# W_k and W_q transposed by blocks of 128 rows, and another order of the work ahead of the first k tile

## The chip, the cores and the metric

The kernel runs on one NeuronCore of a Trainium2 chip. PE (TensorE) does the matmuls and transposes into PSUM, ACT (ScalarE), DVE (VectorE) and POOL (GpSimd) the elementwise work, and SP (SyncE) issues every DMA of this kernel from one queue. The metric is the device time of one execution in microseconds, lower is better. Nine executions of the kernel before gave a median of 279.61 us (279.39 to 280.89).

## The reference

One layer over x of 2048 rows and 640 columns: an attention with a feature map in place of the softmax over keys, then a gated feed-forward block. There are 32 heads of 20 columns.

```python
pq = einsum("bhsd,hdf->bhsf", q, w_phi); pk = einsum("bhsd,hdf->bhsf", k, w_phi)
phi_q = concat([softmax(pq), softmax(-pq)]); phi_k = concat([softmax(pk), softmax(-pk)])
kv = einsum("bhsf,bhsd->bhfd", phi_k, v);  z = einsum("bhsf->bhf", phi_k)
o = einsum("bhqf,bhfd->bhqd", phi_q, kv) / (einsum("bhqf,bhf->bhq", phi_q, z)[..., None] + 1e-6)
h = x + o.reshape(B, S, D) @ wo                              # q, k, v = layernorm(x) @ wqkv
out = h + (gelu(layernorm(h) @ w_gate) * (layernorm(h) @ w_up)) @ w_down
```

## The kernel before

Rows are worked on in 16 tiles of 128 (four tiles make a block of 512; `x_sb[b]` holds one block of x, `LN1T[b]` its normalized transpose). For a tile t the steps are: statistics (`ln_st`, L108 and L112, with the reciprocal deviation on ACT at L117/L118 or on POOL at L120/L121), the normalization `ln_ap` (L137 on DVE, L132 on ACT), the transpose into `LN1T` (`ln_tp`: five PE transposes into PSUM at L145 and a copy at L146; for tiles 6 to 15 a DMA transpose at L148), the v projection (`v_mm`, L260, or its pieces `v_part`, L276; ten matmuls of 128x320) with its copy `v_ev` into `vS` on ACT (L280), and the k projection (`k_tile`, L260) with two exponentials on ACT (L292).

W_k and W_q are not used as they are. `fold` multiplies the weight by a block-diagonal matrix `BD` built from `w_phi`, so that one projection gives pk or pq at once. For this the weight is loaded transposed (`WkT`, `WqT`), six matmuls for each of its five blocks of 128 rows run at L224, and the result is copied to `Wk2` or `Wq2` by ACT (L233) or DVE (L235); the tuples `KA` and `QA` name the blocks that ACT copies. `BD` is one DVE multiplication of `wphi` with the mask `hmask` (L391).

The order on PE and SP is the program's; nothing is reordered there, nor on the other engines, since the whole body stands in a hand-written schedule. Ahead of the loop over tiles (L414) stands a prologue (L374 to L409): tiles 0 to 5 are normalized, tiles 0 to 4 transposed on PE, v is made of tiles 0 to 3, and W_k is folded in two stretches, one in the middle of v of tile 3. In the loop each turn t makes k of tile t and v of tile t + 4; the transposes of tile 5 stand in turn 0 ahead of v of tile 4, and one W_q block is folded in each of the turns 4 to 8 (`FQ`). Tile 3's statistics are made on ACT by two passes (`st3_act`, L357: the squares and the plain sum) and finished on POOL (L359 to L363).

The SP queue begins with x rows by pieces, Wv in three pieces (L174, L176, L177), wphi (L178), then x of tiles 4 and 5 (L179), W_k's transposition as one DMA (L180), x of tiles 6 and 7 (L181), of tiles 8 to 11 (L185), W_q's transposition as one DMA (L186), and x of tiles 12 to 15 (L187). After these come the ten DMA transposes of tiles 6 to 15. [...]

`gtile` takes a PSUM buffer of two banks from a pool of four (three from turn 4 on, with the fourth for `kvp`); a new tile takes the buffer that came free first in the program's order, and its first matmul waits for the last reader of the tile before.

Of the kernel before, what the change touches and what calls it, by code (L numbers as in the profile page):

```python
# [10 lines left out]
ALU = mybir.AluOpType  # L11
# [6 lines left out]
def kernel(  # L18
# [12 lines left out]
    nc = tc.nc  # L31
    P = 128
    S = 2048
    D = 640
    H = 32
    Dh = 20
# [3 lines left out]
    NC = D // P  # L40
# [5 lines left out]
    NH = [(P * c + P - 1) // Dh - H0[c] + 1 for c in range(NC)]  # L46
    NWARM = 10
    VP = (0, 2, 4, 6, 9, 11)
    KA, QA = (0,3), (0,1,2,3,4)
    FQ = (4, 5, 6, 7, 8)  # L50

    QG = ((0, 1), (2, 3), (4, 5), (6,), (7, 8), (9, 10), (11, 12), (13, 14), (15,), (16,), (17,), (18,), (19,))
# [10 lines left out]
    x_v = A_x.rearrange("b (p t) d -> p (b t) d", t=NT)  # L63
    o_v = out.rearrange("b (p t) d -> p (b t) d", t=NT)
    w_v = A_wqkv.rearrange("(c p) n -> p c n", p=P)
    phi_v = A_w_phi.rearrange("h d f -> (h d) f")
# [8 lines left out]
    x_sb = [const.tile([P, 4, D], BF16, name=f"x_sb{b}") for b in range(NB)]  # L75
    wphi = const.tile([P, NC, Dh], BF16, name="wphi")
# [7 lines left out]
    hmask = const.tile([P, NC, 8], BF16, name="hmask")  # L84
    kmask = const.tile([P, NC, 4], BF16, name="kmask")
    BD = const.tile([P, NC, 8, Dh], BF16, name="BD")
# [70 lines left out]
    Wk2 = p1.tile([P, NC, D], BF16, name="Wk2")  # L157
# [16 lines left out]
    nc.sync.dma_start(Wv[:, 0:2, :], w_v[:, 0:2, 2 * D:3 * D])  # L174
    nc.sync.dma_start(x_sb[0][:, 2:3, :], x_v[:, 2:3, :])
    nc.sync.dma_start(Wv[:, 2:4, :], w_v[:, 2:4, 2 * D:3 * D])  # L176
    nc.sync.dma_start(Wv[:, 4:5, :], w_v[:, 4:5, 2 * D:3 * D])  # L177
    nc.sync.dma_start(wphi, phi_v.rearrange("(c p) f -> p c f", p=P))  # L178
    nc.sync.dma_start(x_sb[1][:, 0:2, :], x_v[:, 4:6, :])  # L179
    nc.sync.dma_start_transpose(WkT, A_wqkv[:, D:2 * D])  # L180
    nc.sync.dma_start(x_sb[1][:, 2:4, :], x_v[:, 6:8, :])  # L181
    wo_v = A_wo.rearrange("(c p) n -> p c n", p=P)
    wg_v = B_w_gate.rearrange("(c p) n -> p c n", p=P)
    wu_v = B_w_up.rearrange("(c p) n -> p c n", p=P)
    nc.sync.dma_start(x_sb[2], x_v[:, 8:12, :])  # L185
    nc.sync.dma_start_transpose(WqT, A_wqkv[:, 0:D])  # L186
    nc.sync.dma_start(x_sb[3], x_v[:, 12:16, :])  # L187


    zero = fp.tile([P, 512], BF16, name="zero")  # L190
# [19 lines left out]
    def fold(WT, W2, halves, ds=range(NC)):  # L210


        runs = []
        for c in range(NC):
            lo, hi = H0[c] * Dh, (H0[c] + NH[c]) * Dh
            for u in range(2):
                a, b = max(lo, u * HD), min(hi, (u + 1) * HD)
                if a < b:
                    runs.append((u, c, a, b))
        runs.sort()  # L220
        for d in ds:
            wa = gtile("wa")
            for i, (u, c, a, b) in enumerate(runs):
                nc.tensor.matmul(wa[:, u, a - u * HD:b - u * HD], lhsT=WT[:, c, d * P:(d + 1) * P],  # L224
                                 rhs=BD[:, c].rearrange("p a b -> p (a b)")[:, a - H0[c] * Dh:b - H0[c] * Dh],
                                 start=(i == 0 or runs[i - 1][0] != u),
                                 stop=(i + 1 == len(runs) or runs[i + 1][0] != u), skip_group_check=True)
            dst, src = W2[:, d, :].rearrange("p (u f) -> p u f", u=2), wa[:, :, 0:HD]
            if halves:
                dst = W2[:, d, :].rearrange("p (c u f) -> p u c f", c=NC, u=2)  # L230
                src = src.rearrange("p u (c f) -> p u c f", c=NC)
            if d in (QA if halves else KA):
                nc.scalar.copy(dst, src)  # L233
            else:
                nc.vector.tensor_copy(dst, src)  # L235
# [3 lines left out]
    def ln_st(*tiles, act=True, between=None, log=False):  # L239
        for t, v in zip(tiles, ln_stats(p1, [x_sb[t // 4][:, t % 4, :] for t in tiles], "1", act, between, log)):  # L240
            lnp[t] = v

    def ln_ap(t, on_act=False, on_pe=False):
        ln = (ln_act if on_act else ln_dve)(p1, "1", *lnp[t])
        if on_pe:
            lnp[t] = ln
        else:
            transpose_to(LN1T[t // 4][:, :, t % 4 * P:(t % 4 + 1) * P], ln, False)

    def ln_tp(t, on_dve=False):  # L250
        transpose_to(LN1T[t // 4][:, :, t % 4 * P:(t % 4 + 1) * P], lnp[t], True, on_dve)
# [13 lines left out]
    def v_mm(t, us=(0, 1)):  # L265
        if 0 in us:
            pv[t] = gtile("pv")
        proj(pv[t], t, Wv, us)

    def v_part(t, *cs):  # L270

        if 0 in cs:
            pv[t] = gtile("pv")
        for c in cs:
            for u in range(2):
                nc.tensor.matmul(pv[t][:, u, 0:HD], lhsT=lnT(t, c), rhs=Wv[:, c, u * HD:(u + 1) * HD],  # L276
                                 start=(c == 0), stop=(c == NC - 1))

    def v_ev(t):
        nc.scalar.copy(vS[t % 8][:, :, 0:Dh].rearrange("p (u h) f -> p u h f", u=2),  # L280
                       pv[t][:, :, 0:HD].rearrange("p u (h f) -> p u h f", f=Dh))
# [72 lines left out]
    def st3_act(i):  # L354

        xt = x_sb[0][:, 3, :]
        nc.scalar.activation(sq3, xt, (ACTF.Square, ACTF.Identity)[i], accum_out=sm3[:, i:i + 1])  # L357
        if i == 1:
            nc.gpsimd.tensor_scalar(v3[:, 0:1], sm3[:, 1:2], sm3[:, 1:2], -1.0 / (D * D), op0=ALU.mult, op1=ALU.mult)  # L359
            nc.gpsimd.tensor_scalar_add(v3[:, 0:1], v3[:, 0:1], EPS)  # L360
            nc.gpsimd.tensor_scalar(v3[:, 1:2], sm3[:, 0:1], 1.0 / D, v3[:, 0:1], op0=ALU.mult, op1=ALU.add)
            nc.gpsimd.tensor_tensor(v3[:, 2:3], v3[:, 1:2], nhalf[:, 0:1], op=ALU.pow)
            nc.gpsimd.tensor_scalar(v3[:, 3:4], sm3[:, 1:2], 1.0 / D, None, op0=ALU.mult)  # L363
            lnp[3] = xt, v3[:, 3:4], v3[:, 2:3], None
# [2 lines left out]
    sm3 = fp.tile([P, 2], F32, name="sm3")  # L367
    v3 = fp.tile([P, 4], F32, name="v3")

    def st1_between():  # L370
        st3_act(0)
        ln_ap(0, on_pe=True)

    ln_st(0, act=False, log=True)  # L374
    ln_st(1, act=False, between=st1_between, log=True)
    st3_act(1)
    ln_tp(0, True)
    warm(WA)
    ln_ap(1, on_pe=True)
    v_part(0, 0, 1)  # L380
    ln_tp(1)
    ln_st(2, act=False, log=True)
    v_part(0, 2, 3, 4)
    v_ev(0)
    v_part(1, 0, 1, 2)
    ln_ap(2, on_pe=True)
    ln_ap(3, on_pe=True)
    ln_tp(2, True)
    ln_st(4, act=False)

    nc.vector.tensor_tensor(BD, wphi[:, :, None, :].to_broadcast([P, NC, 8, Dh]),  # L391
                            hmask[:, :, :, None].to_broadcast([P, NC, 8, Dh]), ALU.mult)
    v_part(1, 3, 4)
    v_ev(1)
    v_part(2, 0, 1)
    ln_tp(3)
    v_part(2, 2, 3, 4)
    v_ev(2)
    ln_ap(4, on_pe=True)
    ln_st(5, act=False)  # L400
    v_mm(3, (0,))
    fold(WkT, Wk2, False, (0, 1))
    v_mm(3, (1,))
    v_ev(3)
    fold(WkT, Wk2, False, (2, 3, 4))
    ln_ap(5, on_pe=True)
    ln_tp(4)
    ln_st(6)
    ln_st(7)  # L409
    fp_cm.__exit__(None, None, None)  # L410
    ev_cm = tc.tile_pool(name="ev", bufs=1, side="right", reuse_waits="tile")
# [2 lines left out]
    for t in range(NT):  # L414
        if t == T3:
            ps_cm.close()
            psG = ps_cm.enter_context(tc.tile_pool(name="psG", bufs=3, space=PSUM, reuse_waits="tile"))
            psK = ps_cm.enter_context(tc.tile_pool(name="psK", bufs=1, space=PSUM, reuse_waits="tile"))
            kvp = psK.tile([P, 2, 512], F32, name="kvp")
        k_tile(t)  # L420
        if t == 0:
            ln_tp(5)
            ln_ap(6)
        if t in FQ:
            fold(WqT, Wq2, True, [i for i, f in enumerate(FQ) if f == t])
        for j in range(len(QT)):
            if t == QT[j]:
                q_mm(j)
                q_exp(j)
        if t % 2 == 1 and t >= 5:  # L430
            kv_tile(t - 5)
            kv_tile(t - 4)
        if t + 4 < NT:
            v_mm(t + 4)
        if t > 0 and t + 6 < NT:
            ln_ap(t + 6, on_act=True)
        if t + 4 < NT:
            v_ev(t + 4)
        if t % 2 == 0 and t + 8 < NT:
            ln_st(t + 8, t + 9)  # L440
        k_norm(t)
        if t == 9:
            nc.gpsimd.memset(KV, 0.0)
            nc.gpsimd.memset(kmask, 1.0)
            for r in HALF:
                nc.gpsimd.affine_select(out=kmask[r], in_=kmask[r], pattern=[[4, NC], [-Dh, 4]],
                                        compare_op=ALU.is_ge, fill=0.0, base=0, channel_multiplier=1)
                nc.gpsimd.affine_select(out=kmask[r], in_=kmask[r], pattern=[[-4, NC], [Dh, 4]],
                                        compare_op=ALU.is_ge, fill=0.0, base=Dh - 1, channel_multiplier=-1)
            nc.gpsimd.tensor_copy(KV[:, :, 0, :, KC - 1], kmask)  # L450
            nc.gpsimd.tensor_copy(KV[:, :, 1, :, 0], kmask)
        if t == 10:
            nc.sync.dma_start(Wg, wg_v)
            nc.sync.dma_start(Wo, wo_v)
            nc.sync.dma_start(Wu, wu_v)
# [282 lines left out]
```

The softmax here doesn't subtract the row's maximum and nothing guards it: scores larger than these inputs give would overflow.

## Time and profile before

| | us |
|---|---|
| median of nine executions | 279.61 |
| the profiled execution, time | 279.61 |
| its span (first to last instruction) | 277.9 |
| PE busy | 272.5 (98%) |
| DVE busy | 165.1 (59%) |
| ACT busy | 142.9 (51%) |
| POOL busy | 95.8 (34%) |
| PE busy in the first 24.0 us | 21.52 |
| SP on W_k's transposition; issue to landing | 5.42; 7.4 |
| SP on W_q's transposition; issue to landing | 5.38; 9.0 |
| SP on one 128-row transposition of tiles 6 to 15 | 1.20 |

Busy time of an engine is the sum of its instructions' time without overlaps; matmuls are pipelined and their ends are modelled, so a busy PE can still be waiting a little inside. "Issue to landing" is the time from SP's issue of a DMA to the semaphore that tells that all its data are there. The granted clock of PE was 1.00 in all stretches.

### The profile page before, as it was taken

What the parts mean: (1) busy time and instruction counts of PE and PEld (TensorE: products, weight loads), DVE (VectorE), ACT (ScalarE), POOL (GpSimd) and SP (SyncE); (2) the same over time, 40 slices, a digit from 0 to 9 for tenths busy, and PEclk for the clock granted to TensorE, in tenths of its full rate; (3) what the DMA queues carried; (4) which work ended last, traced back from release to release, by engine and by line L of the source; (5) the groups of instructions that cost most, each with busy time, mean ns of one, the idle gap of its engine ahead of it and who ended that gap; (6) DMA issues with size and microseconds to landing.
All of it is one profiled execution on the core that took longest, in us unless ns stands there. A gap on an engine that the chain in (4) does not pass through costs nothing.

```text
span 277.9 us, 5795 instructions
## 1 busy us (share of the span) xinstructions
PE 272.5 (98%) x2337; PEld 172.1 (62%) x2337; DVE 165.1 (59%) x289; ACT 142.9 (51%) x239; POOL 95.8 (34%) x211
## 2 busy tenths in 40 slices
PE   7999999999999999999999999999999999999995
PEld 2676777764655887788854555675455577444574
DVE  5799998789397776575325757322667532233222
ACT  4669999678597856365524354413446440222200
POOL 3448997685202216355301343400225230000000
PEclk9999999999999999999999999999999999999999
DMA  6996222793530021414120212221031413000011
GB/s 206 243 241 119 51 51 47 191 394 127 162 125 0 4 47 26 93 29 94 26 71 2 47 25 55 42 73 47 5 44 24 74 25 94 26 0 0 0 50 47
DMA packets 40635, 21.05 MB, mean 76 GB/s; under 512 B 33440, under 2 KB 38816, under 8 KB 40608
## 3 DMA queue, kind: packets, MB, share of 16 engines
q1 hardware_dynamic: 40608, 20.68, 29.6%
q8 instruction: 18, 0.29, 0.4%
q14 instruction: 9, 0.07, 0.1%
HBM read 10.18 MB, written 2.62 MB: 46 GB/s over the span
## 4 chain that ended last, share of the span: by engine, by line
PE 90%; DVE 3%; DMA 3%; POOL 1%; ACT 1%; issue 0%; SPq 0%; POOLq 0%
PE gu L588 38%; PE pd L609 19%; PE pq L347 8%; PE po L543 8%; PE pk L260 6%; PE pv L260 5%; PE ab L483 3%; PE kvp L325 2%; DMA LN1T<-ln 2%; DMA x_sb<-in_A_x_dram 1%; DVE stats L108 1%; DVE Wk L235 1%; DVE ln L137 1%; PE wa L224 1%; ACT sq L357 1%
## 5 line engine op out<-in xcount | busy, mean ns | idle before, releaser
L594 DVE TENSOR_TENSOR GT<-gu,g 128x512 bf16<-128x512 f32 (+1 forms) x60 | 34.4, 581 | 54.3 <-ACT g L591 54.1
L591 ACT ACTIVATE g<-gu 128x512 bf16<-128x512 f32 (+1 forms) x60 | 30.8, 513 | 69.3 <-PE gu L588 68.2
L588 PE MATMUL gu<-LN2T,Wg 128*128 128x512 bf16 (+1 forms) x300 | 61.9, 337 | 0.1
L588 PE MATMUL gu<-LN2T,Wu 128*128 128x512 bf16 (+1 forms) x300 | 61.7, 336 | 0.0
L609 PE MATMUL pd<-Wd,GT 128*128 128x320 bf16 (+2 forms) x396 | 53.8, 295 | 0.0
L609 PEld LDWEIGHTS <-GT 128*128 128x128 bf16 x396 | 38.0, 98 | 15.3 <-DVE GT L594 0.9
L588 PEld LDWEIGHTS <-Wu 128*128 128x128 bf16 x300 | 29.4, 98 | 22.6
L588 PEld LDWEIGHTS <-Wg 128*128 128x128 bf16 x300 | 28.4, 98 | 20.7
L260 PEld LDWEIGHTS <-LN1T 128*128 128x128 bf16 x290 | 27.6, 98 | 11.7 <-DMA LN1T<-ln 0.8
L307 POOL TENSOR_TENSOR vt<-vS,rs 128x672 bf16<-128x672 bf16 x22 | 29.7, 1372 | 8.5 <-DVE rs L303 8.0
L614 DVE TENSOR_TENSOR y<-pd,x_sb 128x640 bf16<-128x640 f32 (+3 forms) x18 | 13.5, 750 | 30.2 <-PE pd L609 30.2
L491 ACT COPY AB<-ab 128x704 f32<-128x704 f32 x28 | 19.6, 748 | 19.8 <-PE ab L483 19.6
L299 DVE TENSOR_REDUCE sk<-E 128x64 f32<-128x1280 bf16 x16 | 23.1, 1446 | 3.5 <-ACT E L292 3.5
L524 DVE TENSOR_TENSOR tt<-AB,w 128x1280 bf16<-128x1280 f32 x16 | 23.8, 1486 | 1.1 <-POOL w L517 0.9
L543 PE MATMUL po<-Wo,oT 128*128 128x320 bf16 x160 | 24.3, 299 | 0.0
L292 ACT ACTIVATE E<-pk 128x640 bf16<-128x640 f32 x32 | 20.9, 707 | 6.5 <-PE pk L260 6.3
L260 PE MATMUL pk<-Wk,LN1T 128*128 128x320 bf16 x160 | 24.2, 299 | 0.0
L347 PE MATMUL pq<-LN1T,Wq 128*128 128x512 bf16 x100 | 22.9, 379 | 0.0
L352 ACT ACTIVATE Eq<-pq 128x1024 bf16<-128x1024 f32 (+1 forms) x26 | 19.9, 829 | 2.4 <-PE pq L347 2.4
L260 PE MATMUL pv<-Wv,LN1T 128*128 128x320 bf16 x130 | 20.0, 299 | 0.5 <-DMA LN1T<-ln 0.5
L543 PEld LDWEIGHTS <-oT 128*128 128x128 bf16 x160 | 15.6, 98 | 7.0 <-ACT oT L146 0.3
L132 ACT ACTIVATE ln<-x_sb,v,rstd 128x640 bf16<-128x640 bf16 x14 | 12.9, 919 | 11.3 <-POOL v L571 11.1
(89 smaller groups left out, 263.1 us busy)
## 6 DMA issues: line engine op xcount, KB each, us to landing
out_dram<-y SPq DMA_DIRECT2D x15, 160.0 KB, 1.8
Wg<-in_B_w_gate_dram SPq DMA_DIRECT2D x1, 1920.0 KB, 7.8
Wu<-in_B_w_up_dram SPq DMA_DIRECT2D x1, 1920.0 KB, 15.0
Wd<-in_B_w_down_dram SPq DMA_DIRECT2D x1, 1920.0 KB, 7.9
x_sb<-in_A_x_dram SPq DMA_DIRECT2D x2, 640.0 KB, 5.4
Wo<-in_A_wo_dram SPq DMA_DIRECT2D x1, 800.0 KB, 9.4
x_sb<-in_A_x_dram SPq DMA_DIRECT2D x4, 160.0 KB, 3.0
Wv<-in_A_wqkv_dram SPq DMA_DIRECT2D x2, 320.0 KB, 4.2
```

What stands on the lines that cost most here:

```text
L260: nc.tensor.matmul(ps[:, u, 0:HD], lhsT=lnT(t, c), rhs=W[:, c, u * HD:(u + 1) * HD], start=(c == 0), stop=(c == NC - 1))
L292: nc.scalar.activation(Ek[t][:, s, :].rearrange("p (u f) -> p u f", u=2), pk[:, :, 0:HD], ACTF.Exp, scale=(1.0 if s == 0 else -1.0))
L299: nc.vector.reduce_sum(sk, Ek[t].rearrange("p s (h f) -> p (s h) f", f=Dh), axis=AX.X)
L307: eng.tensor_tensor(vt[:, s], vS[t % 8], rs[:, s * H:(s + 1) * H, None].to_broadcast([P, H, VC]), ALU.mult)
L347: nc.tensor.matmul(pqs[j][:, i, :], lhsT=Wq2[:, kc, c * P:(c + 1) * P], rhs=LN1T[b][:, kc, :], start=(kc == 0), stop=(kc == NC - 1))
L352: nc.scalar.activation(Eq[j][:, :, s, :], pqs[j][:, 0:len(QG[j])], ACTF.Exp, scale=(1.0, -1.0)[s])
L524: nc.vector.tensor_tensor(tt.rearrange("p s (h f) -> p s h f", f=Dh), num, w[:, :, :, None].to_broadcast([P, 2, H, Dh]), ALU.mult)
L543: nc.tensor.matmul(po[:, u, 0:HD], lhsT=st[t][:, c, :], rhs=Wo[:, c, u * HD:(u + 1) * HD], start=(c == 0), stop=(c == NC - 1))
L588: nc.tensor.matmul(gu[:, i, 0:n], lhsT=W[:, c, f * P:(f + 1) * P], rhs=LN2T[b][:, c, a0:a1], start=(c == 0), stop=(c == NC - 1))
L591: nc.scalar.activation(g[:, 0:n], gu[:, 0, 0:n], ACTF.Gelu_apprx_tanh)
L594: nc.vector.tensor_tensor(st[b, "g", f][:, a0:a1], gu[:, 1, 0:n], g[:, 0:n], ALU.mult)
L609: nc.tensor.matmul(pd[:, u, n0:n1], lhsT=st[b, "g", f][:, tl * P:(tl + 1) * P], rhs=Wd[:, f, u * HD + n0:u * HD + n1], start=(f == 0), sto ...
```

## The change

wphi is loaded ahead of the third piece of Wv. W_k and W_q are transposed by five DMAs of 128 rows each (`load_T`). The loads of x of tiles 6 and 7, 8 to 11 and 12 to 15 are issued after all of W_k; three W_q blocks stand between the last two of them, the fourth W_q block is issued behind tile 6's transpose and the fifth in turn 1, ahead of tile 7's. `BD` is made in two pieces, block columns 0 to 2 and 3 to 4 (`bd`), before and after the normalization of tile 2. The two ACT passes of tile 3 move behind the reciprocal deviations of tiles 1 and 2, and the normalization of tile 3 behind the statistics of tile 4. v of tile 2 is made in one stretch, then W_k's blocks 0 to 2 are folded, tile 3 is transposed, blocks 3 and 4 are folded, and v of tile 3 is made in one stretch; ACT copies blocks 1 and 3 instead of 0 and 3. Tile 5 is transposed behind v of tile 4.

```diff
-    KA, QA = (0,3), (0,1,2,3,4)
+    KA, QA = (1,3), (0,1,2,3,4)
...
     nc.sync.dma_start(Wv[:, 2:4, :], w_v[:, 2:4, 2 * D:3 * D])
+    nc.sync.dma_start(wphi, phi_v.rearrange("(c p) f -> p c f", p=P))
     nc.sync.dma_start(Wv[:, 4:5, :], w_v[:, 4:5, 2 * D:3 * D])
-    nc.sync.dma_start(wphi, phi_v.rearrange("(c p) f -> p c f", p=P))
     nc.sync.dma_start(x_sb[1][:, 0:2, :], x_v[:, 4:6, :])
-    nc.sync.dma_start_transpose(WkT, A_wqkv[:, D:2 * D])
-    nc.sync.dma_start(x_sb[1][:, 2:4, :], x_v[:, 6:8, :])
+
+    def load_T(WT, i, *ds):
+
+        for d in ds:
+            nc.sync.dma_start_transpose(WT[:, :, d * P:(d + 1) * P], A_wqkv[d * P:(d + 1) * P, i * D:(i + 1) * D])
+
+    load_T(WkT, 1, *range(NC))
...
-    nc.sync.dma_start(x_sb[2], x_v[:, 8:12, :])
-    nc.sync.dma_start_transpose(WqT, A_wqkv[:, 0:D])
-    nc.sync.dma_start(x_sb[3], x_v[:, 12:16, :])
...
-    def st1_between():
-        st3_act(0)
-        ln_ap(0, on_pe=True)
+    def bd(c0, c1):
+
+        n = c1 - c0
+        nc.vector.tensor_tensor(BD[:, c0:c1], wphi[:, c0:c1, None, :].to_broadcast([P, n, 8, Dh]),
+                                hmask[:, c0:c1, :, None].to_broadcast([P, n, 8, Dh]), ALU.mult)
 
     ln_st(0, act=False, log=True)
-    ln_st(1, act=False, between=st1_between, log=True)
-    st3_act(1)
+    ln_st(1, act=False, between=lambda: ln_ap(0, on_pe=True), log=True)
+    st3_act(0)
     ln_tp(0, True)
     warm(WA)
     ln_ap(1, on_pe=True)
     v_part(0, 0, 1)
     ln_tp(1)
     ln_st(2, act=False, log=True)
+    st3_act(1)
     v_part(0, 2, 3, 4)
     v_ev(0)
+    bd(0, 3)
+    ln_ap(2, on_pe=True)
+    bd(3, NC)
     v_part(1, 0, 1, 2)
-    ln_ap(2, on_pe=True)
-    ln_ap(3, on_pe=True)
     ln_tp(2, True)
     ln_st(4, act=False)
-
-    nc.vector.tensor_tensor(BD, wphi[:, :, None, :].to_broadcast([P, NC, 8, Dh]),
-                            hmask[:, :, :, None].to_broadcast([P, NC, 8, Dh]), ALU.mult)
+    ln_ap(3, on_pe=True)
     v_part(1, 3, 4)
     v_ev(1)
-    v_part(2, 0, 1)
-    ln_tp(3)
-    v_part(2, 2, 3, 4)
+    v_part(2, *range(NC))
     v_ev(2)
+    nc.sync.dma_start(x_sb[1][:, 2:4, :], x_v[:, 6:8, :])
+    nc.sync.dma_start(x_sb[2], x_v[:, 8:12, :])
+    load_T(WqT, 0, 0, 1, 2)
+    nc.sync.dma_start(x_sb[3], x_v[:, 12:16, :])
+    fold(WkT, Wk2, False, (0, 1, 2))
+    ln_tp(3, False)
+    fold(WkT, Wk2, False, (3, 4))
+    v_mm(3)
+    v_ev(3)
     ln_ap(4, on_pe=True)
+    ln_tp(4)
     ln_st(5, act=False)
-    v_mm(3, (0,))
-    fold(WkT, Wk2, False, (0, 1))
-    v_mm(3, (1,))
-    v_ev(3)
-    fold(WkT, Wk2, False, (2, 3, 4))
+    ln_st(6)
     ln_ap(5, on_pe=True)
-    ln_tp(4)
-    ln_st(6)
     ln_st(7)
...
         if t == 0:
-            ln_tp(5)
             ln_ap(6)
+            load_T(WqT, 0, 3)
+        if t == 1:
+            load_T(WqT, 0, 4)
...
         if t + 4 < NT:
             v_mm(t + 4)
+            if t == 0:
+                ln_tp(5)
```

## The prediction

> **What bounds the kernel now.** I read the busy table of the whole span first, then PE by stretches, then the chain of waits in order of time, then the single waits of the stretch that has any.
>
> ```profile
> 0.00:24.00 24.00, 21.52 (x163) 13.26 (x164) 19.39 (x52) 16.01 (x30) 10.67 (x39) 1.00 0.95 221
> 24.00:48.00 24.00, 24.00 (x295) 17.97 (x294) 22.55 (x38) 22.14 (x36) 20.98 (x25) 1.00 0.28 54
> ...
> 19.01 0.44 DVE ln L137
> 19.45 0.03 DVE stats L108
> 19.48 4.24 DMA LN1T<-ln
> 23.72 0.05 issue
> 23.76 1.53 PE pv L260 x10
> 25.29 1.36 PE pk L260 x10
> ```
>
> The first two lines give length, then busy time of PE, PEld, DVE, ACT and POOL, granted clock, DMA share, GB/s. From 24 us on PE never idles, and the chain from 23.76 is PE alone, 1.36 us for each group of ten 128x320 matmuls. Before 23.76 it runs through DMA, ACT, POOL and DVE. The change touches only instructions ahead of that point, two DMAs behind it, and the PSUM buffers. So its worth is by how much earlier PE begins the v of tile 6 (now 23.76) plus what it adds behind. All times "now" are starts in the trace; those of the changed kernel I work out by following each wait with these durations.
>
> ```profile
> 15.89 1.70 PE L260 MATMUL pk<-Wk,LN1T 128*128 128x320 bf16 x10
> 17.43 0.44 PE L145 MATMUL tp<-ident,ln 128*128 128x128 bf16 x5
> 17.71 1.52 PE L260 MATMUL pv<-Wv,LN1T 128*128 128x320 bf16 x10
> 19.07 1.52 PE L260 MATMUL pk<-Wk,LN1T 128*128 128x320 bf16 x10
> ...
> 23.76 0.45 PE L260 MATMUL pv<-Wv,LN1T 128*128 128x320 bf16 x2 [0.46 <-DMA LN1T<-ln]
> ...
> 26.69 1.30 ACT L292 ACTIVATE E<-pk 128x640 bf16<-128x640 f32 x2 [0.66 <-PE pk L260]
> 27.88 0.92 ACT L132 ACTIVATE ln<-x_sb,mr,rstd 128x640 bf16<-128x640 bf16 x1
> 28.68 0.70 ACT L280 CAST vS<-pv 128x640 bf16<-128x640 f32 x1
> ```
>
> k of tile 0 holds PE from 15.89 to 17.43, 1.54 us where 1.36 are needed: its fifth operand, the last Wk copy on DVE, comes at 16.56. Then v4, k1, v5, k2 follow without a gap, the last due to end at 21.78 + 1.36 = 23.14; PE waits 0.62 us more for the transposed tile 6, which landed at 23.72. That DMA took 4.24 us where most of the ten take 2.57, since it stands behind the 640 KB load of x rows 12 to 15, landed at 23.19, itself behind W_q's transposition, landed at 20.70.
>
> **The change part by part.**
>
> *wphi ahead of the last Wv piece.* The v of tile 0 follows the Wv loads closely: its third pair of matmuls begins at 7.56 (second piece landed 7.52), its fifth at 8.13 (third piece, issued 3.64, landed 8.09). wphi is 640 runs of 40 B. From 6.4 to 8.0 the DMA engines are full, and a 40 B packet takes 10 ns in the packet records: 640 x 0.010 / 16 = 0.40 us ahead of Wv. Bounds: 0 if they slip in beside; 1.5 us, the stretch over which wphi's packets lie now. I take 0.40, by the packets' own time: fifth pair at 8.53. Of that 0.31 stays: PE does the pair and three more of tile 1 (8 x 0.135) and reaches the transposes of tile 2 at 9.61 instead of 9.30, where it now waits for ln of tile 2 anyway.
>
> The Trainium skill ("DMA: Bandwidth & Descriptors", Specifications) gives 512 B as the least transfer for line rate, which speaks against a 40 B load ahead of a needed one. [...]
>
> *Block diagonals in two pieces, squares of tile 3 later.* Now one DVE instruction of 0.94 us for 800 elements at 11.24. The pieces, 480 and 320, cost by the same rate 0.56 and 0.38. The first fits into DVE's 0.67 us wait before ln of tile 2 (8.13 to 8.80), wphi being there by about 7.9; the second ends near 9.5, before the copy of tile 2 is due. Nothing on the path; without the cover 0.6. The squares (0.83 us each with their read) move behind the rstd of tiles 1 and 2: POOL's statistics of tile 3, 1.9 us, end at 11.4 instead of 9.33. Queued behind them is the rstd of tile 4 (to 12.6, used at 15); ln of tile 3 ends at 12.1, and PE wants it at 12.97. Cover 0.9 us.
>
> *The order on PE.* Transposes of tile 2 at 9.61, copy 0.49, v of tile 2 at 10.65 (now 10.34) and in one stretch to 12.02. Folds 0 to 2 at 0.315 each end at 12.97; their buffers are free (vS of tile 0 is copied by 10.1, of tile 1 by 11.3). Transposes of tile 3 at 12.97; on ACT vS of tile 2 (12.2), a Wk copy (12.8), LN1T of tile 3 (13.45 to 14.14, 0.69 each, 0.6 when back to back). Folds 3 and 4 wait for the DVE copy of fold 0 (13.30) and end at 13.98. Then PE waits for LN1T of tile 3: v of tile 3 at 14.20. It ends at 15.57, transposes of tile 4 (0.28) to 15.85, k of tile 0 there: 0.04 earlier than now. The last Wk copy is done at 15.0, so k takes 1.36: 17.21. v4 follows (its LN1T copied at 17.04), transposes of tile 5 18.57, k1, v5, k2 end at 22.93. This is 0.21 earlier than the 23.14 of now.
>
> *W_k in five pieces.* The five transposed blocks hold the bytes of the one DMA (5.42 us of SP). By the 1.20 us that SP spends on each 128-row transposition: starts from 5.20 every 1.25 us, the last at 10.20, landing 2.57 later at 12.8, while fold 4 comes at 13.67. The packets now come in full rate after 9.5 and reach 640, 1280, ... by 9.4, 10.2, 10.8, 11.3, 11.9; landing about 0.6 later, they are 0.8 to 1.5 us ahead of each fold. Does each piece wait for the one before? The two transpositions that SP issued at 217.53 and 219.20 landed 0.51 apart, so no.
>
> The skill's rule on many small transfers (same page, Rules for kernel authors: coalesce them) speaks against five pieces; with its fitted fixed 2.0 us, which it gives for another issuing engine, five in series would end near 17.1 as an estimate by the page, and the sum would be about 3.4 us slower. No row here shows such a series.
>
> *x and W_q on SP.* The loads of x rows 6 and 7 and of 8 to 11 are issued at 11.45 and 12.07 (now 10.66, 11.28); they land after W_k anyway (now W_k 12.63, then 14.26 and 16.10), so about 14.4 and 16.3, used at 16.3 and 19. Three W_q blocks instead of five stand before x rows 12 to 15: 1920 packets instead of 3200 at 1136 per us save 1.1 us, and x rows 12 to 15 land near 21 to 22. Tile 6's transposition, issued at 19.3 behind its ln, then lands between 21.9 (2.57 alone) and 22.7: before 22.93. The 0.62 us wait is gone; if it stayed late, up to that comes back. The last two W_q blocks are put between it and tile 7's: SP 20.55, 21.80, tile 7 at 23.05 instead of 22.75, landing 25.62. PE wants it at 22.93 + 2.72 = 25.65. Level; the cover of 1.1 us that it has now is spent.
>
> *A PSUM buffer.* Buffers are given out in the order of release. Followed through both listings, the first W_q fold (tile 4) now takes the buffer of v of tile 6, then that of v of tile 7. It waits for that vS copy: E of tile 3 begins 0.20 after PE's end of k3 and the copy ends 2.89 after it (26.49 to 29.38); PE, with v7 and k4, is there 2.72 after. Wait: 29.43 - 29.20 = 0.23. Later folds find the buffers as now.
>
> *Sum.* 22.93 - 23.76 = -0.83, and +0.23: -0.60. The profiled execution took 279.61 us with a span of 277.9 (1.7 lie around it), and 279.61 is also the median of the nine runs. 279.61 - 0.60 = 279.0.
>
> **Rivals.** (a) wphi costs Wv nothing. For it: 25 KB beside 160; against: the engines are full in that stretch. Then everything from 9.61 on is 0.31 earlier: 278.7. (b) The expected gain is lost at tile 6: an instruction fetch of 16 KB, which fell at 18.1 and again at 30.9 in this trace, each time with a transposition landing 1.2 to 1.8 late, falls in the W_q blocks, or Wv comes later than I take it (up to 1.5 instead of 0.40). Tile 6 then lands 23.1 to 23.5: 279.2 to 279.6; I take 279.4, no change. (c) The other side: tile 7's transposition, now third in a row on SP, lands late. Of the ten LN1T ones three took 4.20 to 4.36 instead of 2.57. With 1.79 more it lands at 27.4, PE starts v7 1.76 late, the buffer's 0.23 is then covered: -0.83 + 1.76 = +0.9, 280.5. It decides from a landing at 26.45, where v7 begins now. Against it: no fetch fell between 21.7 and 30.9. The steeper end of Wv's delay (+1.1 on the sum) also gives +0.5.
>
> **How the numbers follow.** A measurement of this kernel can tell about 0.2% (0.56 us) from no change. Forecast, 278.7 to 279.3: 0.50, of which 0.35 under 279.05. (a), 278.0 to 278.7: 0.14. (b), within 0.2%: 0.17. (c) and Wv's far end: 0.19. So faster 0.49, same 0.32, slower 0.19. The range from 278.1 to 280.5 leaves out the tails of (a) and (c).
>
> **What would show it.** Right: fifth pair of v0 at 8.5; no PE wait on W_k; k0 near 15.85 and 1.36 us long; tile 6 landed before 22.9; a wait of 0.2 before the first W_q fold. Wrong: folds waiting for W_k's pieces, a wait at v of tile 6 or 7 in the chain, Wv landing at 8.1 or past 9, or a PE gap after 30 us.

## The result and the profile after

The changed kernel takes 280.55 us (median of 19 runs, 279.95 to 281.44) against 279.51 for the kernel before (median of 62 runs): ratio 1.0032, interval 1.0022 to 1.0042. It is slower by about 0.9 us, where 0.6 us of gain was forecast. A second batch gave 1.0027 (1.0015 to 1.0040). Among the runs below, one of a_best2 took 405.11 us at a granted clock of 0.658; the ratios leave it out.

The profiled execution of the changed kernel took 281.44 us, span 279.7 (before: 279.61, span 277.9). It lies above its own median, so I profiled the same kernel once more (281.12 us, span 279.4) and quote both where they differ. The second lies above the median of its batch too (280.53), so both show about 0.6 to 0.9 us more of a loss than the median execution has.

First PE by stretches, as before: length, then busy time of PE, PEld, DVE, ACT and POOL, granted clock, DMA share, GB/s.

```profile
0.00:24.00 24.00, 20.94 (x161) 13.42 (x161) 18.92 (x53) 15.28 (x29) 9.86 (x38) 1.00 0.98 206
24.00:48.00 24.00, 22.96 (x256) 16.95 (x258) 22.25 (x37) 21.60 (x33) 21.34 (x24) 1.00 0.32 65
48.00:80.00 32.00, 32.00 (x432) 20.07 (x431) 23.76 (x32) 23.33 (x33) 17.21 (x19) 1.00 0.69 218
```

PE idles 1.04 us in 24 to 48, where before it idled nowhere, and the DMA engines moved fewer GB/s in the first 24 us (206, before 221) while they were busy for more of it. From 48 to 80 PE is full at clock 1.00. The chain of waits (start, length, what) puts the loss ahead of 31 us, but for one wait at 205 us:

```profile
4.16 5.22 DMA Wv<-in_A_wqkv_dram
...
9.42 1.25 PE pv L278 x8
...
20.18 4.76 DMA LN1T<-ln
...
24.98 1.53 PE pv L262 x10
...
28.51 0.70 ACT E L294
29.21 0.81 ACT ln L132
30.02 0.59 ACT vS L282
...
30.65 0.47 PE wa L226 x6
```

Three things stand in it: the last Wv piece, landed at 9.38 (8.09 before); the transposed tile 6, issued at 20.18 and landed 4.76 later, for which v6 starts at 24.98 (23.76 before); and the copy of vS ahead of the first W_q fold. PE's timeline (start, length, what, and in brackets the idle time before it) of the same stretch:

```profile
22.43 1.52 PE L262 MATMUL pk<-Wk,LN1T 128*128 128x320 bf16 x10
24.98 1.53 PE L262 MATMUL pv<-Wv,LN1T 128*128 128x320 bf16 x10 [1.03 <-DMA LN1T<-ln]
26.35 1.52 PE L262 MATMUL pk<-Wk,LN1T 128*128 128x320 bf16 x10
27.71 1.52 PE L262 MATMUL pv<-Wv,LN1T 128*128 128x320 bf16 x10
29.07 1.52 PE L262 MATMUL pk<-Wk,LN1T 128*128 128x320 bf16 x10
30.65 0.47 PE L226 MATMUL wa<-BD,WqT 128*128 128x140 bf16 x6
```

A start less the start before it gives the step: 1.36 for a group of ten, so k2 was due to end at 22.43 + 1.36 = 23.79 and v6 waited 1.19 (the 1.03 in brackets goes by a modelled end). v7 follows without a wait; the fold waits 30.65 - 29.07 - 1.36 = 0.22. In the second profile k2 ends at 23.30, v6 starts at 24.51 after a wait of 1.21, and the fold waits 0.22 again:

```profile
21.93 1.52 PE L262 MATMUL pk<-Wk,LN1T 128*128 128x320 bf16 x10
24.51 1.53 PE L262 MATMUL pv<-Wv,LN1T 128*128 128x320 bf16 x10 [1.05 <-DMA LN1T<-ln]
```

Behind that both kernels keep a fixed distance up to 200 us: +1.44 in the first profile, +0.97 in the second. At 205 us each profile loses another 0.40 and 0.54 to one transposition of `o`, of which more at the end.

Why is tile 6 late? SP's own timeline (start, length, what it issued), first of the kernel before, then of the changed one:

```profile
5.20 5.42 SPq L180 DMA_TRANSPOSE WkT<-in_A_wqkv_dram  x1
10.66 0.57 SPq L181 DMA_DIRECT2D x_sb<-in_A_x_dram  x1
11.29 0.42 SPq L185 DMA_DIRECT2D x_sb<-in_A_x_dram  x1
11.76 5.38 SPq L186 DMA_TRANSPOSE WqT<-in_A_wqkv_dram  x1
17.18 0.58 SPq L187 DMA_DIRECT2D x_sb<-in_A_x_dram  x1
```

```profile
5.20 7.46 SPq L184 DMA_TRANSPOSE WkT<-in_A_wqkv_dram  x5
12.70 0.58 SPq L401 DMA_DIRECT2D x_sb<-in_A_x_dram  x1
13.33 0.42 SPq L402 DMA_DIRECT2D x_sb<-in_A_x_dram  x1
13.80 4.60 SPq L184 DMA_TRANSPOSE WqT<-in_A_wqkv_dram  x3
18.44 1.16 SPq L404 DMA_DIRECT2D x_sb<-in_A_x_dram  x1
20.18 1.21 SPq L148 DMA_TRANSPOSE LN1T<-ln  x1
```

Five pieces of W_k hold SP for 7.46 us instead of 5.42, and all that follows is issued 2 us later. The landings in the trace carry that through:

| landed at, us | before | after | after, second profile |
|---|---|---|---|
| Wv, last piece | 8.09 | 9.38 | 8.76 |
| W_k, all | 12.63 | 14.49 | 14.12 |
| x rows 6, 7 | 14.26 | 16.35 | 16.36 |
| x rows 8 to 11 | 16.10 | 20.04 | 18.10 |
| W_q, what is issued ahead of x 12 to 15 | 20.70 | 22.04 | 21.58 |
| x rows 12 to 15 | 23.19 | 24.34 | 23.89 |
| tile 6 transposed | 23.72 | 24.93 | 24.46 |

Each row lands behind the row above it. Tile 6 lands 0.5 to 0.6 us behind x rows 12 to 15 in every column, whenever it was issued (19.48, 20.18 and 19.76). Its own issue does not set its landing: 2.57 us, which such a transposition takes alone, behind 20.18 would be 22.75, before k2 ends.

Not all of the 2 us on SP is the pieces' own. Where the last Wv piece landed by 8.35 (a_wphi, b_wk5, a_wphi_wq, a_wqlate_vs below), the five pieces held SP for 6.57 to 6.63; where it landed at 8.76, 8.90 and 9.38, for 6.85, 6.98 and 7.46. So 1.2 us come with the pieces alone (6.6 less 5.42), and 0.2 to 0.9 more go with a late Wv.

### The profile page after: what moved, and what is told of

The parts are those of the page before. It is cut to its first block, busy times and chain, and to the rows that moved or that the text cites. A ratio compares the mean times of both kernels' runs of the same rounds, so it can differ in the third digit from the quotient of the medians.

```text
span 279.7 us, 5808 instructions
## 1 busy us (share of the span) xinstructions
PE 272.5 (97%) x2337; PEld 172.4 (62%) x2337; DVE 165.4 (59%) x290; ACT 143.1 (51%) x239; POOL 95.6 (34%) x211
## 4 chain that ended last, share of the span: by engine, by line
PE 89%; DMA 5%; DVE 2%; SPq 1%; ACT 1%; issue 1%
PE gu L598 36%; PE pd L619 19%; PE pq L349 8%; PE po L553 8%; PE pk L262 6%; PE pv L262 5%; PE ab L493 2%; PE kvp L327 2%; DMA Wv<-in_A_wqkv_dram 2%; DMA LN1T<-ln 2%; DMA oT<-o 1%; PE wa L226 1%; PE pv L278 1%; DVE stats L108 1%; PE tp L145 1%
```

## The experiments

Three theories. Q: the end is set by the transposed tile 6, which stands on SP's queue behind W_k's pieces, x and W_q. W: the late Wv is what is paid. F: chance in the execution (an instruction fetch) sets it. The first four kernels take one part of the change away, or make one part alone. All diffs are against the changed kernel, or against the kernel before where that is said.

**wphi behind Wv again (a_wphi).**

```
-    nc.sync.dma_start(wphi, ...)
     nc.sync.dma_start(Wv[:, 4:5, :], w_v[:, 4:5, 2 * D:3 * D])
+    nc.sync.dma_start(wphi, ...)
```

> The changed kernel with wphi issued behind the last Wv piece again, all else as changed. Theory Q (the end is set by the transposed tile 6, which stands on SP behind W_k's pieces, x and W_q): the fifth pair of v0 begins 0.5 to 0.9 us earlier (8.5 to 8.9 instead of 9.42), k2 ends 0.3 to 0.8 earlier, but tile 6 still lands near 24.9 and v6 still begins there: 280.5, ratio to before 1.002 to 1.004. Theory W (the late Wv is what is paid): v6 begins 0.6 to 0.8 earlier, 279.7 to 279.9. Theory F (an instruction fetch or other chance of the execution sets the end): tile 6 lands at another time without any order of SP being changed.

Measured: 280.12 us, ratio 1.0020 (1.0004 to 1.0037). Wv landed at 8.21, k2 was due to end at 23.20, tile 6 landed at 23.67 and v6 started at 23.72, a wait of 0.51. The time lies between Q and W, and so does the trace: the wait at v6 is still there, as Q has it, but tile 6 came earlier than Q said, since x rows 8 to 11 landed at 17.20. SP is free of W_k at 11.83 here, at 12.66 and 12.05 in the two profiles of the change. So wphi's place may well be part of the loss, through the queue; that is not shown, since the intervals of the two kernels overlap.

**W_k as one DMA again (a_wk1).**

```
-    load_T(WkT, 1, *range(NC))
+    nc.sync.dma_start_transpose(WkT, A_wqkv[:, D:2 * D])
```

> The changed kernel with W_k's transposition as one DMA again, all else as changed. Theory Q: SP is free 2.0 us earlier (10.7 instead of 12.7), x rows 6 to 11 and the W_q blocks land 1.5 to 2 us earlier, tile 6 near 22.9 to 23.5, the wait of 1.19 at v6 shrinks to 0 to 0.2, v6 at 23.8 to 24.0: 279.3 to 279.6. The first fold is not later, since W_k landed whole at 12.63 and the first fold begins at 12.90. Theory W: no change, 280.5. Theory F: no change beyond the scatter.

Measured: 279.77 us, ratio 0.9998 (0.9982 to 1.0014). SP and PE of this kernel:

```profile
5.20 5.33 SPq L186 DMA_TRANSPOSE WkT<-in_A_wqkv_dram  x1
...
19.93 1.20 SPq L148 DMA_TRANSPOSE LN1T<-ln  x1
21.17 2.60 SPq L184 DMA_TRANSPOSE WqT<-in_A_wqkv_dram  x2
23.87 3.19 SPq L148 DMA_TRANSPOSE LN1T<-ln  x2
```

```profile
22.18 1.52 PE L262 MATMUL pk<-Wk,LN1T 128*128 128x320 bf16 x10
23.54 1.52 PE L262 MATMUL pv<-Wv,LN1T 128*128 128x320 bf16 x10
24.89 1.52 PE L262 MATMUL pk<-Wk,LN1T 128*128 128x320 bf16 x10
26.57 1.53 PE L262 MATMUL pv<-Wv,LN1T 128*128 128x320 bf16 x10 [0.16 <-DMA LN1T<-ln]
27.94 1.52 PE L262 MATMUL pk<-Wk,LN1T 128*128 128x320 bf16 x10
29.30 0.48 PE L226 MATMUL wa<-BD,WqT 128*128 128x140 bf16 x6
```

SP is free at 10.53, x rows 12 to 15 land at 21.04, tile 6 at 22.49, and v6 follows k2 with no wait. Now tile 7 is late: behind two W_q blocks it is issued at 23.87 and lands at 26.52, v7 waits 0.32, and with that the fold waits no more. Q is right that the wait at v6 goes; it did not have the one at v7, and the time lies 0.2 above its upper end. W, which had no change here, is not right: Wv landed at 8.80, as late as in the second profile of the change.

**W_q behind the transposed tiles (a_wqlate).**

```
     nc.sync.dma_start(x_sb[2], x_v[:, 8:12, :])
-    load_T(WqT, 0, 0, 1, 2)
     nc.sync.dma_start(x_sb[3], x_v[:, 12:16, :])
...
             ln_ap(6)
-            load_T(WqT, 0, 3)
-        if t == 1:
-            load_T(WqT, 0, 4)
...
             ln_ap(t + 6, on_act=True)
+        if t < NC:
+            load_T(WqT, 0, t)
```

> The changed kernel with all five W_q blocks moved behind the transposed tiles 6, 7, 8, 9 and 10, one behind each (the fold of a block comes four tiles later), W_k in five pieces as changed. Theory Q: nothing but x rows 8 to 15 stands ahead of tile 6; x rows 12 to 15 land 2 to 3 us earlier (21.5 to 22 instead of 24.34), tile 6 near 22.8, no wait at v6, v6 at 23.8: 279.3. Theory W: no change, 280.5. If the new blocks make tile 7 or 8 late instead, a wait at v7 or v8 of up to 1 us shows.

Measured: 279.64 us, ratio 0.9995 (0.9981 to 1.0010). With W_k in five pieces and Wv late (8.90) as in the change:

```profile
19.71 1.21 SPq L148 DMA_TRANSPOSE LN1T<-ln  x1
20.96 1.27 SPq L184 DMA_TRANSPOSE WqT<-in_A_wqkv_dram  x1
```

```profile
23.32 1.52 PE L262 MATMUL pv<-Wv,LN1T 128*128 128x320 bf16 x10
24.68 1.52 PE L262 MATMUL pk<-Wk,LN1T 128*128 128x320 bf16 x10
26.04 1.52 PE L262 MATMUL pv<-Wv,LN1T 128*128 128x320 bf16 x10
27.39 1.52 PE L262 MATMUL pk<-Wk,LN1T 128*128 128x320 bf16 x10
28.98 0.47 PE L226 MATMUL wa<-BD,WqT 128*128 128x140 bf16 x6
```

Tile 6 lands 2.58 after its issue (22.28), and neither v6 nor v7 waits. The fold's wait is back: 28.98 - 27.39 - 1.36 = 0.23. With it and with 0.35 at 205 us the time lies 0.3 above the 279.3 of Q.

**W_k in five pieces alone, on the kernel before (b_wk5).**

```
-    nc.sync.dma_start_transpose(WkT, A_wqkv[:, D:2 * D])
+    for d in range(NC):
+        nc.sync.dma_start_transpose(WkT[:, :, d * P:(d + 1) * P], A_wqkv[d * P:(d + 1) * P, D:2 * D])
```

> The kernel before with one edit: W_k's transposition in five pieces of 128 rows. Theory Q: the pieces hold SP for 7.5 instead of 5.4 us and land 1.9 later as a whole (14.5); x rows 6 to 15 and W_q behind them land about 2 us later, tile 6 near 25 to 25.7, v6 about 1.2 to 1.9 later than the 23.76 of before: 280.7 to 281.4, ratio 1.004 to 1.007. Theory W: Wv is not touched, so no change: 279.5. Theory F: no change beyond the scatter.

Measured: 282.69 us, ratio 1.0091 (1.0057 to 1.0125), more than Q's upper end. SP spent 6.57 on the pieces, W_k landed whole at 14.20, x rows 12 to 15 at 24.84, tile 6 at 25.65. PE, then the stretches around it:

```profile
21.99 1.52 PE L261 MATMUL pk<-Wk,LN1T 128*128 128x320 bf16 x10
25.69 1.95 PE L261 MATMUL pv<-Wv,LN1T 128*128 128x320 bf16 x10 [2.18 <-ACT ln L132]
27.44 2.82 PE L261 MATMUL pk<-Wk,LN1T 128*128 128x320 bf16 x10
30.09 1.52 PE L261 MATMUL pv<-Wv,LN1T 128*128 128x320 bf16 x10
```

```profile
23.00:26.00 3.00, 0.82 (x7) 0.37 (x6) 2.96 (x5) 2.62 (x4) 2.64 (x3) 1.00 0.92 249
26.00:30.00 4.00, 4.00 (x20) 2.43 (x18) 3.71 (x8) 0.69 (x1) 3.48 (x7) 0.58 0.21 41
```

The wait at v6 is 25.69 - 21.99 - 1.36 = 2.34; it is the transposition's, which landed at 25.65, although the bracket names an ACT instruction that ended close to it. What Q did not have is the second step: after this gap PE's granted clock is 0.58 from 26 to 30, v6 and k3 take 1.75 and 2.65 instead of 1.36, and 1.7 us go there. Not every execution pays that step: three of the six had a mean granted clock of 0.994 and took 283.15 to 283.47, the other three had 1.00 and took 281.19 to 282.24. Even these are 1.6 us and more above the kernel before. So one edit, with Wv untouched, makes the kernel before slower by more than the whole change does. That is against W and F, which had no change here.

The second four test the sum of the parts. First the changed kernel once more, unaltered (after_again).

> The changed kernel once more, unaltered, for a second profile. Theory V (its first profile, 281.44 us against a median of 280.55, showed an execution with late loads: two variants with the same queue up to there had the last Wv piece at 8.8 to 8.9 and x rows 8 to 11 at 16.0 to 17.9 where it has 9.38 and 20.04): now Wv 8.8 to 9.0, x rows 8 to 11 near 18, tile 6 at 23.9 to 24.5, v6 0.3 to 0.9 later than the 23.76 of before, 280.3 to 280.7. Theory S (the first profile is the rule): 9.4, 20.0, 24.9 and a span near 279.5. In both, the time goes to the wait at v6, and the wait of about 0.2 before the first W_q fold stands unless v7 is late.

Measured: 280.53 us, 1.0027 (1.0015 to 1.0040), span 279.4; the landings are in the table above. V holds for Wv, x and tile 6. The span holds S's number, since this execution lost 0.54 at 205 us.

**W_q behind the transposed tiles, on the kernel before (b_wqlate).** The same place of W_q as in a_wqlate, in five pieces, with W_k whole and everything else as before.

> The kernel before with one edit: W_q's transposition taken out of its place between the x loads and given in five blocks of 128 rows, one behind each of the transposed tiles 6 (or 7) to 11, four tiles ahead of the fold that reads it. Theory Q: x rows 12 to 15 land by 18.5 to 19.5 instead of 23.19, tile 6 2.6 after its issue (22.1), no wait at v6: v6 at 23.14 instead of 23.76, less the wait of 0.2 before the first fold if that turns up here too: 278.9 to 279.2, ratio 0.998 to 0.999. If what the change gains is its PE order, this gains nothing: 279.5.

Measured: 279.23 us, ratio 0.9977 (0.9963 to 0.9990). x rows 12 to 15 landed at 17.72, tile 6 at 22.35, v6 started at 23.42 with no wait, and the fold did not wait either. The wait of 0.62 at v6, which the change was to remove, goes by giving this one transposition later and in pieces.

**Both edits on the changed kernel (a_wphi_wq)**: wphi behind Wv and W_q behind the transposed tiles.

> The changed kernel with wphi behind Wv again and with the W_q blocks behind the transposed tiles: the two edits of the earlier runs together. Theory Q: Wv at 8.2, k2 ends near 23.2, tile 6 at 22.3, so v6 at 23.2 instead of 23.76; the wait of 0.22 before the first W_q fold comes back, since v7 isn't late: -0.56 + 0.22 = -0.34, 279.2, ratio 0.9988. If tile 7 is late (it landed 25.53 where it would be wanted at 25.9), 0 to 0.2 more. Rival: the two edits overlap (both only take away the wait at v6), then 279.6 as with the W_q blocks alone.

Measured: 279.54 us, ratio 0.9991 (0.9980 to 1.0002). v6 at 23.11, no wait at v6 or v7, and a wait of 0.22 at the fold: -0.44 for PE up to 200 us, near the -0.34 of Q. The interval doesn't tell it from the rival's 279.6.

**The best version (a_best)**: those two edits, W_k in two pieces, and vS of tile 7 copied ahead of ln of tile 9.

```
-    load_T(WkT, 1, *range(NC))
+    for d0, d1 in ((0, 3), (3, NC)):
+        nc.sync.dma_start_transpose(WkT[:, :, d0 * P:d1 * P], A_wqkv[d0 * P:d1 * P, D:2 * D])
...
+        if t == 3:
+            v_ev(t + 4)
         if t > 0 and t + 6 < NT:
             ln_ap(t + 6, on_act=True)
...
-        if t + 4 < NT:
+        if t + 4 < NT and t != 3:
             v_ev(t + 4)
```

> As a_wphi_wq, with W_k in two pieces (384 and 256 rows) instead of five, and with vS of tile 7 copied by ACT ahead of ln of tile 9 instead of behind it. Expected by theory Q: SP spends 5.5 on W_k instead of 6.7, the second piece lands near 13 instead of 14.04, folds 3 and 4 do not wait (v3 0.3 earlier than with five pieces), v6 at 22.8 to 23.2; the copy of vS of tile 7 ends 0.8 earlier, so no wait before the first W_q fold: -0.6 to -0.9 altogether, 278.6 to 279.0, ratio 0.9965 to 0.998. If the fold's wait was not that copy, 0.2 of it stays.

Measured: 278.81 us, ratio 0.9966 (0.9954 to 0.9978), faster than both kernels (the changed one has 1.0015 to 1.0040 in the same batch). SP, then PE:

```profile
5.19 5.19 SPq L187 DMA_TRANSPOSE WkT<-in_A_wqkv_dram  x2
...
19.23 1.21 SPq L148 DMA_TRANSPOSE LN1T<-ln  x1
```

```profile
22.84 1.52 PE L263 MATMUL pv<-Wv,LN1T 128*128 128x320 bf16 x10
...
26.91 1.52 PE L263 MATMUL pk<-Wk,LN1T 128*128 128x320 bf16 x10
28.27 0.48 PE L227 MATMUL wa<-BD,WqT 128*128 128x140 bf16 x6
```

Two pieces hold SP for 5.19, no longer than one; v6 starts at 22.84, and the fold follows k4 after exactly 1.36. Against b_wqlate, which has W_k whole and the order of before, v6 is 0.58 earlier (23.42 - 22.84, one profile each): that is what the change's order on PE is worth together with W_k in two pieces, once tile 6 lets it through. The times say less: 0.9966 against 0.9977, with intervals that overlap.

SP is free at 10.38 here, as early as with one piece, and W_k landed at 12.94; yet x rows 6 and 7 landed at 15.35, against 14.02 in b_wqlate, whose queue differs only in W_k. So it is not the time on SP alone that moves the loads behind W_k: the pieces' own landing, or what else is in flight, has a part that these runs do not separate.

The repetition of a_best (a_best2) was expected thus:

> a_best once more, unaltered: 278.6 to 279.0, ratio 0.9955 to 0.998; the fold follows k4 without a wait, v6 at 22.8.

It gave 278.92 us, ratio 0.9965 (0.9945 to 0.9985). Where v6 and the fold lie in it is not known.

The last three price single terms. **wphi ahead of Wv on the kernel before (b_wphi)**, the same two lines of the diff as in the change:

> The kernel before with one edit: wphi ahead of the last Wv piece. In the ten profiles so far the last Wv piece landed at 8.09 to 8.27 with wphi behind it and at 8.76 to 9.38 with wphi ahead. Theory Q: Wv lands 0.5 to 0.7 later (8.7 to 8.9), PE reaches the transposes of tile 2 about 0.3 later and k2 ends about 0.3 later, but tile 6 lands where it did (23.7), so v6 stays at 23.8: no change, 279.5, ratio 1.000. Theory W (Wv's delay is paid in full): +0.3, ratio 1.001 or more.

Measured: 279.63 us, ratio 0.9994 (0.9972 to 1.0016): no change that can be told. But the profiled execution (280.62 us) was one in which Wv landed at 9.86, so late that k2 ended at 24.81, after tile 6 had landed at 24.71; there Wv, not tile 6, was paid, +1.04 for PE, as W has it.

**wphi ahead of Wv in the best version (a_best_wphi).**

> a_best with wphi ahead of the last Wv piece, as in the change. Here no transposed tile is late, so the same delay of Wv is on the path: tp of tile 2 at 9.9 instead of 9.54, v6 0.3 to 0.4 later (23.1 to 23.2): 279.1 to 279.2, ratio 0.9975 to 0.998. If wphi's place costs nothing even here, 278.8.

Measured: 279.09 us, ratio 0.9963 (0.9945 to 0.9982). Wv landed at 8.57, v6 started at 22.98, 0.14 later than in a_best. The medians differ by 0.2 to 0.3, but the ratios (0.9963 against 0.9966 and 0.9965) do not differ: that wphi's place costs time here is seen in one profile and not shown by the times.

**vS of tile 7 first, in the kernel with W_q behind (a_wqlate_vs)**, the last hunk of a_best alone on a_wqlate:

> a_wqlate (27.39 + 1.36 = 28.75 is where k4 ended, and the first W_q fold began at 28.98) with one more edit: ACT copies vS of tile 7 ahead of ln of tile 9. If the fold's wait is that copy's, as predicted, it is gone and PE is 0.2 earlier from there on, 0.45 ahead of before: 279.3 to 279.4 by the medians, ratio 0.9984. If the wait belongs to another buffer, it stays, or it moves to v8 or the second fold.

Measured: 279.21 us, ratio 0.9978 (0.9958 to 0.9997). k4 starts at 27.01 and the fold at 28.37, 1.36 later: the wait is gone, and neither v8 nor the second fold took it over. It was that copy's, as predicted.

## Why the prediction was wrong

The sum was -0.83 + 0.23. Of the -0.83, 0.21 was an earlier end of k2 and 0.62 the wait at v6. Measured in the second profile, k2 ends 0.16 later (23.30 instead of 23.14) and v6 waits 1.21 instead of 0.62: +0.75; and +0.22 at the fold. In the first profile k2 ends 0.65 later, v6 waits 1.19 and the fold 0.22.

- **The step that failed: "x and W_q on SP".** It said that tile 6 "lands between 21.9 (2.57 alone) and 22.7: before 22.93. The 0.62 us wait is gone". It landed at 24.46 and 24.93, and PE waited 1.2 us where the sum had nothing. The saving by three W_q blocks instead of five was right: 3.5 us from the landing of x rows 8 to 11 to that of W_q in the second profile, 4.6 before. What it was counted from was wrong: in the second profile x rows 6 and 7, 8 to 11 and 12 to 15 landed 1.8 to 2.9 us after the times set for them. Taking W_q out of the queue ahead of it (a_wqlate) brings it to 22.28 and takes the wait away; so does giving W_k as one DMA (a_wk1), to 22.49.
- **Its root is the step before it, "W_k in five pieces".** It took 1.20 to 1.25 of SP for a piece and 2.57 to land, the last at 12.8. The pieces held SP for 6.85 and 7.46, and the last landed at 14.12 and 14.49, 3.36 us after its issue in the second profile. I checked that figure only against the fold that reads the piece, where 0.9 us of cover made it look harmless, and then set x rows 6 and 7 "about 14.4" as if it held. They land 1.5 to 2.4 us behind W_k in every profile: 16.36. b_wk5 shows that the five pieces alone are enough to make tile 6 late; in the change SP's time on them was longer still, along with a late Wv, as above.
- The skill's rule on many small transfers (the Trainium skill, "DMA: Bandwidth & Descriptors", Rules for kernel authors) spoke against the pieces and was set aside; b_wk5, 1.0091, agrees with its sign. Its size, as the prediction worked it out, does not show: in all profiles with five pieces W_k landed at 13.8 to 14.5, not near 17.1.
- **wphi ahead of Wv** was taken at 0.40, bounds 0 to 1.5, from 10 ns a packet; in the trace the median of these packets is 11 ns, which would make it 0.44. Over seven profiles with wphi ahead Wv landed at 8.35 to 9.86 (median 8.80), over six with wphi behind at 8.09 to 8.28 (median 8.22): 0.6 in the middle, and a scatter that reached past the bound. In the two profiles of the change it is 1.29 and 0.67 against the 8.09 of before. At v6 that delay is hidden, since tile 6 lands after k2 ends in both; if it counts, it is through the queue, as above.
- **The order on PE** was right to 0.1 us once Wv is allowed for. In the second profile the fifth pair of v0 begins 0.28 late (8.81 instead of 8.53), v3 0.30 (14.50 instead of 14.20) and k0 0.37 (16.22 instead of 15.85); k0 is 1.36 long, as predicted. A wait on W_k, which was ruled out, did come: fold 4 waited 0.2 for the last piece, but v3 waited for the copy of LN1T until 14.40 anyway. With Wv in time it shows more: in a_wphi fold 4 begins at 14.08, when the piece is there, and v3 at 14.41, where a_best with two pieces has 14.12.
- **Block diagonals and squares** cost nothing on the path of the change, although the two pieces took 0.66 and 0.48 instead of 0.56 and 0.38. With wphi behind Wv they do: in a_wphi the first piece waits 0.36 for wphi and holds the normalization of tile 2, so the transposes of tile 2 begin at 9.58 instead of 9.30.
- **The buffer's wait** was right: 0.22 and 0.22 for 0.23, and a_wqlate_vs shows its cause.
- **The rivals.** (b) named the place, tile 6, but put its end at "no change", by a fetch or a late Wv; the queue alone did more. (c) gave the time, 280.5, but by luck: it had tile 7 land late, and in the change v7 does not wait, because v6 is already late. In a_wk1, where tile 6 is in time, tile 7 does come 0.32 late, but by its issue at 23.87 behind two W_q blocks (23.05 was predicted): it took 2.65 to land, not the 4.36 of (c).

One thing stays open: the 0.40 and 0.54 at 205 us. They lie in one transposition of `o`, issued near 201, which took 3.92 and 4.07 to land, with an instruction fetch of 16 KB beside it; in the kernel before it took 3.39 with such a fetch, and PE did not wait. Six of the other seven profiles of kernels with the change's order (a_best2 left out) show 0.2 to 0.5 there, a_wk1 does not; none of the four with the order of before does. The packet records say how the two go together: in all 13 of these profiles this transposition landed 1.53 to 1.60 us after the fetch ended. The fetch ended 1.5 to 1.9 us after the issue in the five profiles that lose nothing there and 2.1 to 2.5 after it in the eight that lose, and PE asks for the tile 3.57 after the issue. Why the fetch comes later beside it with the change's order stays open.

## What to carry to other kernels

A DMA that is split into pieces is to be priced by the queue that issues it: take the time until that queue is free and the landing of the last piece, and follow both through every transfer behind, to the one that sets the end, and not only to the reader of the pieces. Where a transposition of the inner loop stands behind large loads, move the loads whose readers are far away (W_q, read eight microseconds later) behind it: alone this gave 0.9977. The reordering of the compute showed a gain only together with it (0.9966 with W_k in two pieces and the copy of vS first); how the gain divides among these is not separated. A cover that is spent by one edit (tile 6) shows the next wait in row (tile 7, then the buffer): work out two or three of them before a sum is made.

## What the runs showed of the hardware

- Five 128-row transpositions of one weight held SP for 6.6 to 7.5 us, one whole 5.2 to 5.4 (6.4 for W_k in b_wphi, where Wv was late, and 7.1 for W_q in b_wk5, behind the five pieces), two pieces 5.2 to 5.4.
- Behind a copy on the same queue a transposed tile of 160 KB landed 0.5 to 0.8 us after that copy in all six profiles where the copy landed 3.0 to 4.2 us after the tile's issue. In the other profiles, where the copy landed at most 1.4 us after the issue or before it, the tile took 2.56 to 2.59 from its issue.
- A PE gap of 2.34 us in b_wk5 was followed by a granted clock of 0.58 over the next 4 us; gaps of 1.19 and 1.21 left it at 1.00. The Trainium skill ("TensorE: Matmul & The Clock Gate", Part 1: The HAM clock gate (the "warmup" mystery)) puts the drop after an idle window of about 3.4 us that runs freely; here a gap shorter than that window was followed by the drop. Three of the six executions of b_wk5 show it in their mean granted clock (0.994, the others 1.00); how long the gap was in the five that were not profiled is not known.
